# An attention stage whose order is set by tables of positions, with two stretches of value products and no mask products

## The chip, the cores and the metric

The kernel runs on one core of one Trainium2 chip. The metric is the device time of one execution in microseconds, as the median over the runs shown. A profiled execution of the same kernel gives the trace from which all rows below come.

## The reference, cut to what matters

One block of a transformer for 2048 positions of width 512 is computed, with modulation of its norms and gates by a condition vector:

```
h = layernorm(x) * (1 + ca) + sa
q, k, v = split(h @ wqkv)                 # 32 heads of 16
s = q @ k.T * 16**-0.5
s = where(0 <= i - j < 256, s, -1e9)      # i query, j key
x = x + ga * (softmax(s) @ v) @ wo
h = layernorm(x) * (1 + cb) + sb
x = x + gb * (silu(h @ w1) * (h @ w3)) @ w2
```

Each query sees itself and the 255 positions before it. With blocks of 128 positions, a query block meets three key blocks: its own (where later keys are masked), the one before it (whole), and the one before that (where only the part inside the window counts).

## The kernel before, in words

The work has three parts: a start (first norm, projections of the values, modulation), the attention, and the feed-forward part. The attention is done in 32 units. A unit `u = 4 g + b` stands for a group `g` of four heads and a block `b` of 512 positions. Each unit has three pieces, which are done for different units at the same time:

- `unit_a` projects queries and keys for unit `u`: twelve products `pj` (high and low parts of the numbers are multiplied apart, for precision), three copies out of PSUM by ScalarE (`out`), two subtractions by GpSimd (`mix`, L430), and six DMAs (`rows`) that put the parts into `ring`, the tile from which all scores are taken.
- `unit_b` finds the row maxima: sixteen products (L466, bank `mx`), each followed on VectorE by an add of a mask and a maximum in one instruction (`top`, L473), then `parts`, a `turn` on TensorE (L488), a copy (`cut`) and two DMAs that put the maxima into `ring` as further rows. The score products of `unit_c` so subtract the maximum by themselves.
- `unit_c` takes scores again with keys on the partitions: sixteen products (L717, bank `st`), for four key blocks `j`, two pairs `a` of heads and two heads `hh` in each. ScalarE exponentiates them into `pt`. Then `values_of` (L693) multiplies with the values into the bank `po`, which is copied out (L782) and stored. Since a key block serves queries of the next unit too, the products of `j` 2 and 3 have a late portion, which is done in the next unit.

There are eight PSUM banks: three `st`, three `mx`, one `pj`, one `po`.

The mask of a pair of heads is put on in one of four ways, by a letter of `MODE` at place `2 j + a`:

- E: TensorE adds the masks, by a second product of an identity with a tile of masks (L720), 256 columns wide or 128.
- D: VectorE adds the masks to the scores in PSUM (L725).
- C: VectorE copies, by a predicate, the third block's scores over the first block's masked half (`merge`, L735), since the two triangles fit together; ScalarE exponentiates two blocks instead of three (L738); GpSimd parts the merged block into two with two selects (`part`, L745).
- P: ScalarE copies the masked blocks to SBUF (`side`, L752), GpSimd masks them there (L762), ScalarE exponentiates them.

C becomes D where a key block meets fewer than three query blocks, which is so for `j` 2 and 3 at `b = 3`. The last three units take `MODL` instead of `MODE`.

The order of all steps of the attention is written by hand: every step is given a position in units of an eighth of a unit, `at(t, fn)`, and the list is sorted by position. So the positions do not set times, only the order in which each engine is given its instructions. A unit has eight positions, unit `u` of `unit_c` starts at `8 u`, `unit_a` of `u` at `8 (u - 3) + X["oa"]`, and `unit_b` at `8 (u - 2) + X["ob"]`. Beside the units run jobs (`jobs`: scaled or summed weights, a load, an operation on GpSimd, a store).

From position `TS` = 229.9 on, steps of the attention stand as fixed steps in a planner (`Sched`), which puts the work of the feed-forward part around them and behind them, by estimated durations and the keys that the constants `K` give. The planner sees the fixed steps with the durations of `KINDS`.

Of the kernel before, what the change touches and what calls it, by code (L numbers as in the profile page):

```python
# [28 lines left out]
X = dict(hh=0.184, ra=0.382, ev=(0.407, 0.03, 0.229), mix=(0.805, 0.86), row=(0.832, 0.887, 2.192), tl=0.402, mr=(0.161, 0.359, 1.088), c=(0.363, 1.109, 2.176, 0.003, 0.321, 1.738), pv=4.377, o=(0.115, 0.58), oa=-0.975, ob=1.274)  # L29
MODE = 'CECPCECP'  # L30
# [216 lines left out]
KINDS = dict(scores=("PE", 0.2), top=("DVE", 0.5), parts=("DVE", 0.4), turn=("PE", 0.11), cut=("ACT", 0.16),  # L247
# [3 lines left out]
JOB = (-1.5, 2.2, 7.9)  # L251
# [6 lines left out]
K = dict(be=(('DVE', 'POOL'), ('DVE', 'POOL'), ('DVE', 'POOL'), ('DVE', 'POOL'), ('DVE', 'POOL'),  # L258
         ('POOL', 'POOL'), ('DVE', 'POOL')), hr=9.016, de=18.699, wo=0.403, x1=3.432, xb=-3.473,
         xl=0.573, os=0.346, ol=(-6.127, -2.69, 14.829, 4.08), pl=(10.986, -0.476, -6.236,  # L260
         31.344), pe=(5.042, -12.993, 12.016, 237.531), o=(3.133, 8.773, 14.919, 2.52), n=(1, 1,
         1, 1), w0=0.71, l2=1.803, f=4.032, fl=41.71, by=((('POOL', 'POOL'), ('DVE', 'DVE'),
         ('DVE', 'POOL'), ('POOL', 'DVE')), (('POOL', 'DVE'), ('POOL', 'POOL'), ('DVE', 'POOL'),
         ('DVE', 'POOL')), (('DVE', 'DVE'), ('POOL', 'DVE'), ('POOL', 'DVE'), ('DVE', 'POOL')),
         (('POOL', 'POOL'), ('DVE', 'DVE'), ('POOL', 'POOL'), ('DVE', 'POOL'))), w=-0.242,
         dn=0.504, ds=0.172, l3=-112.914)
@with_exitstack
def block_kernel(ctx: ExitStack, tc: tile.TileContext, x, wqk, wv, wo, w13, w2, c, wmod, out):
# [183 lines left out]

    def unit_b(u, t0, at):
# [49 lines left out]
        t1 = t0 + 8 + X["tl"]
        at(t1, parts, "parts")
        at(t1 + X["mr"][0], turn, "turn")
        at(t1 + X["mr"][1], out, "cut")
        at(t1 + X["mr"][2], rows, "rows")
# [189 lines left out]
    def unit_c(u, t0, at):  # L697
# [12 lines left out]
        def scores(j, a, hh):  # L710
            kb = 4 * b + j
            nq, nm, bl = blks(j)
            if hh == 0:
# [3 lines left out]
            nc.tensor.matmul(ps[:, :nq], keys(NM, hh, a, kb, 1), queries(NM, a, kb, nq),  # L717
                             start=True, stop=not plus)
            if plus:
                nc.tensor.matmul(ps[:, bl], identr, mskr[:, :nm], start=False, stop=True)  # L720
# [740 lines left out]
    kb_ = [us(8 * (NU - NB + b) + 6 + X["pv"] + X["o"][1]) for b in range(NB)]  # L1461
# [103 lines left out]
```

## Time and profile before

| | us |
|---|---|
| median of 3 runs | 1018.6 |
| lowest, highest | 1018.1, 1021.03 |
| profiled execution | 1016.29 |
| span of the profiled execution | 1014.6 |

| engine | busy us | share of the span | instructions |
|---|---|---|---|
| TensorE (products) | 976.0 | 96% | 5432 |
| TensorE (weight loads) | 721.6 | 71% | 5432 |
| VectorE | 697.9 | 69% | 1878 |
| ScalarE | 562.3 | 55% | 1252 |
| GpSimd | 594.8 | 59% | 736 |

The mean granted clock of TensorE was 0.993. The attention lasts from about 100 to 520 us of the span; the last copy of a unit out of PSUM starts at 519.6 us. In rows of the profile PE is TensorE, PEld its weight loads, DVE VectorE, ACT ScalarE, POOL GpSimd, SP the queue that issues DMAs. A row of the timeline gives start, duration, engine, line, operation, output and inputs with their shapes, and a count; the duration of a product goes to its modelled end, so that products overlap in the rows and the distance between starts is what one takes of TensorE.

### The profile page before, as it was taken

The page shows a single profiled execution, that of the slowest core. Times are in us where ns is not written, and L with a number is a line of the kernel's source. Part 1 is how long each engine was busy: PE and PEld are TensorE (multiplying, and loading weights), DVE is VectorE, ACT ScalarE, POOL GpSimd, SP SyncE. Part 2 cuts the span into 40 slices and gives each one's busy share as a digit, 9 for nine tenths or more (in the row PEclk, how much of TensorE's full clock was granted, in tenths as well). Part 3 has the DMA queues.
Part 4 walks back from the last instruction along what each step waited for, and adds up shares of the span by engine and source line. Part 5 has one row for each costly group of instructions (what it writes and reads, how often), then busy time and mean ns, then how long its engine had stood idle before and what let it go on. Part 6 is the DMA issues. An engine that isn't in the chain of part 4 may idle for free.

```text
span 1014.6 us, 17251 instructions
## 1 busy us (share of the span) xinstructions
PE 976.0 (96%) x5432; PEld 721.6 (71%) x5432; DVE 697.9 (69%) x1878; ACT 562.3 (55%) x1252; POOL 594.8 (59%) x736
## 2 busy tenths in 40 slices
PE   5999999999999999999888899999999999999998
PEld 2578666666666666666456688878888788888886
DVE  7775777777878787878546875566577755665555
ACT  3433777777776777776557766344345444333330
POOL 7341766666665757564548677787786754433420
PEclk9999999999999999999999999999999999999999
DMA  8521353434353434335466066665556343222102
GB/s 296 161 84 43 100 173 125 143 124 144 124 173 123 143 125 148 120 134 173 161 204 221 23 239 195 219 223 193 170 162 194 130 129 93 67 84 66 49 22 83
DMA packets 79983, 141.65 MB, mean 140 GB/s; under 512 B 9234, under 2 KB 22034, under 8 KB 79764
## 3 DMA queue, kind: packets, MB, share of 16 engines
q1 hardware_dynamic: 79172, 139.50, 42.2%
q10 hardware_dynamic: 720, 1.05, 0.3%
q8 instruction: 43, 0.70, 0.3%
q14 instruction: 48, 0.39, 0.1%
HBM read 85.72 MB, written 34.61 MB: 119 GB/s over the span
## 4 chain that ended last, share of the span: by engine, by line
PE 82%; DVE 7%; ACT 4%; DMA 4%; issue 1%; POOL 1%; SPq 0%; POOLq 0%; ACTq 0%; DVEq 0%
PE st L1341 11%; PE mx L1341 11%; PE pj L412 9%; PE mx L466 9%; PE po L693 8%; PE st L717 8%; PE mx L1434 6%; PE st L1434 6%; PE st L631 4%; PE pj L1434 3%; PE pj L1341 3%; PE st L720 1%; PE mx L1079 1%; DMA o_dr<-os 1%; DVE hT L329 1%
## 5 line engine op out<-in xcount | busy, mean ns | idle before, releaser
L473 DVE CUSTOM_DVE_ANT_0 junk<-mx,mskq 128x384 bf16<-128x384 f32 (+2 forms) x512 | 267.5, 528 | 54.2 <-PE mx L466 50.4
L466 PE MATMUL mx<-ring 96*128 96x384 f32 (+2 forms) x512 | 172.9, 351 | 3.9 <-DVE mt L473 2.0
L717 PE MATMUL st<-ring 100*128 100x384 f32 (+2 forms) x512 | 157.1, 343 | 5.7 <-DMA ring<-mT 3.4
L412 PE MATMUL pj<-hT,wq 128*128 128x512 f32 x384 | 153.8, 416 | 1.5 <-DVE hT L329 1.2
L745 POOL TENSOR_SCALAR_AFFINE_SELECT pt<-pt 128x256 f32<-128x256 f32 x224 | 91.4, 413 | 94.5 <-ACT pt L738 86.8
L466 PEld LDWEIGHTS mx<-ring 96*128 96x128 f32 x512 | 94.7, 190 | 61.9 <-DVE mt L473 41.3
L934 POOL TENSOR_TENSOR w<-w,w 128x512 fp32r<-128x512 f32 (+2 forms) x56 | 98.0, 1758 | 56.5 <-ACT w L933 54.2
L738 ACT ACTIVATE pt<-st 128x256 f32<-128x256 f32 x224 | 85.4, 395 | 54.6 <-DVE st L735 53.2
L717 PEld LDWEIGHTS st<-ring 100*128 100x128 f32 x512 | 96.8, 191 | 19.4 <-ACT pt L738 6.6
L693 PE MATMUL po<-pt,vS 128*17 128x384 f32 (+2 forms) x1408 | 108.5, 393 | 0.0
L430 POOL TENSOR_TENSOR qk<-qkr,qk 128x512 fp32r<-128x512 f32 x64 | 82.3, 1286 | 42.6 <-ACT qkr L418 39.4
L729 ACT ACTIVATE pt<-st 128x384 f32<-128x384 f32 (+2 forms) x172 | 77.3, 457 | 37.8 <-PE st L720 32.9
L735 DVE COPY_PREDICATED st<-later,st 128x128 f32<-128x128 uint8 x224 | 65.2, 293 | 46.6 <-PE st L717 46.3
L412 PEld LDWEIGHTS pj<-hT,wq 128*128 128x128 f32 x384 | 72.2, 190 | 26.2 <-issue 17.8
L1372 DVE TENSOR_TENSOR t<-mx,t 128x512 f32<-128x512 f32 x51 | 35.1, 689 | 54.4 <-PE mx L1341 44.5
L1384 POOL TENSOR_TENSOR t<-t,t 128x512 f32<-128x512 f32 x28 | 36.2, 1293 | 58.6 <-DVE t L1372 56.1
L1412 ACT ACTIVATE wq<-g 128x512 fp32r<-128x512 f32 x28 | 17.7, 634 | 92.6 <-DVE g L1368 63.6
L1341 PE MATMUL st<-b,w 128*128 128x512 f32 x264 | 65.9, 392 | 0.6 <-DVE b L1238 0.6
L1372 DVE TENSOR_TENSOR t<-st,t 128x512 f32<-128x512 f32 x50 | 34.3, 688 | 45.8 <-PE st L1341 38.8
L1341 PE MATMUL mx<-b,w 128*128 128x512 f32 x258 | 63.7, 391 | 1.7 <-ACT t L1375 0.9
L1341 PEld LDWEIGHTS mx<-b,w 128*128 128x128 f32 x258 | 48.4, 188 | 12.8 <-ACT t L1375 1.3
L1341 PEld LDWEIGHTS st<-b,w 128*128 128x128 f32 x264 | 49.2, 188 | 11.5 <-DVE b L1238 1.1
(274 smaller groups left out, 2102.4 us busy)
## 6 DMA issues: line engine op xcount, KB each, us to landing
ring<-qk SPq DMA_DIRECT2D x192, 128.0 KB
o_dr<-os SPq DMA_DIRECT2D x32, 256.0 KB
w<-wsum SPq DMA_DIRECT2D x14, 512.0 KB
w<-w2g SPq DMA_DIRECT2D x14, 512.0 KB
jb<-in_w SPq DMA_DIRECT2D x24, 256.0 KB
wraw<-in_w SPq DMA_DIRECT2D x7, 768.0 KB
w<-wraw SPq DMA_DIRECT2D x14, 384.0 KB
vS<-in_wmod SPq DMA_DIRECT2D x20, 256.0 KB
```

Source lines behind the costliest of these rows:

```text
L412: nc.tensor.matmul(v["ps"], WQ[g][w][:, n // 3], hTp(i, n // 3, b * BT, BT), start=(n == 0), stop=(n == 3 * KC - 1))
L430: nc.gpsimd.tensor_tensor(out=v[n], in0=v["raw"], in1=v[1].bitcast(F32), op=ALU.subtract)
L466: nc.tensor.matmul(v[i][:, :n], queries(NS, a, gq, 1), keys(NS, hh, a, k0, gq + 1 - k0), start=True, stop=True)
L473: nc.vector.tensor_tensor_reduce(out=junk[:, :n], in0=v[i][:, :n], in1=mskq[:, 3 * P - n:], scale=1.0, scalar=-3e38, op0=ALU.add, op1=ALU. ...
L693: nc.tensor.matmul(po[32 * i:32 * i + DH + 1, qb * P:(qb + nq) * P], vS[:, kb, 4 * g + i], pts[i // 2][:, i % 2, c0:c0 + nq], start=first, ...
L717: nc.tensor.matmul(ps[:, :nq], keys(NM, hh, a, kb, 1), queries(NM, a, kb, nq), start=True, stop=not plus)
L729: nc.scalar.activation(held[u, j, a][:, hh, :nq], v[j, a, hh][:, :nq], AF.Exp, scale=SCALE)
L738: nc.scalar.activation(held[u, j, a][:, hh, :2], v[j, a, hh][:, :2], AF.Exp, scale=SCALE)
L745: nc.gpsimd.affine_select(out=pt[:, :, 2 * m], in_=pt[:, :, 0], **w)
L934: sch.op(eng, lambda: on_eng(eng).tensor_tensor(out=lo(), in0=src(), in1=hi().bitcast(F32), op=ALU.subtract), 0.06 + 0.0024 * n if eng == ...
L1341: nc.tensor.matmul(ps(bk), WT[s, n][w][:, col], BB[t, k][r], start=start and c == 0, stop=stop and c == 5, skip_group_check=True)
L1434: nc.tensor.matmul(ps(bk), tiles[hk + (h,)][:, i * P:(i + 1) * P], w2_of(last, y, f), start=(m == 0), stop=(m == 5))
```

## The change

All steps of the three pieces are placed by tables with one position for each step, in place of steps at even distances. `X` holds the tables of the attention's main part, `Y` those of the steps that are done in the start; `Y` repeats the old positions. `MODE` changes in two places: pair `j0 a1` goes from E to D, pair `j2 a1` from E to C. `MODL` stays, so the last three units keep their products L720. The products with the values of a unit stand in two groups: the late ones of the unit before together with `j` 0, and `j` 1, 2 and 3. Since the two heads of a pair can come in either order now, the tiles are taken by whichever comes first. The planner knows more of the steps (`KINDS`), waits with the tiles `qkr` and `qk` until the last rows are sent, and has new constants `K`.

```diff
-X = dict(hh=0.184, ra=0.382, ev=(0.407, 0.03, 0.229), mix=(0.805, 0.86), row=(0.832, 0.887, 2.192), tl=0.402, mr=(0.161, 0.359, 1.088), c=(0.363, 1.109, 2.176, 0.003, 0.321, 1.738), pv=4.377, o=(0.115, 0.58), oa=-0.975, ob=1.274)
-MODE = 'CECPCECP'
+X = dict(oa=-1.228, ob=1.317, wqk=(-2.382, 3.131, 4.551), pj=(-1.966, -1.918, -1.881, -0.877, -0.359, -0.355,
+         -0.265, 0.076, 1.497, 3.335, 3.917, 4.363), ev=(4.727, 5.775, 5.259), mix=(5.588, 6.021),
+         row=(8.681, 8.806, 9.018), mx=(0.546, 0.669, 1.455, 2.0, 2.064, 2.307, 2.929, 2.957, 3.255, 4.081,
+         4.688, 5.039, 6.139, 6.215, 6.787, 7.106), tl=(0.31, 0.576, 0.39, 0.716, 0.354, 0.742, 0.497, 1.151,
+         0.762, 0.785, 0.491, 0.953, 0.338, 1.726, 1.317, 1.105), mr=(8.575, 8.773, 9.063, 9.269), st=(1.873,
+         1.594, -2.503, 2.891, 0.05, 3.409, 2.644, 3.504, 4.618, 4.477, 4.419, 5.916, 5.311, 7.665, 6.691,
+         6.671), c=(0.385, 0.805, 2.402, 0.573, 0.759, 1.126), pv=(4.115, 8.948, 9.091, 9.582, 3.792, 4.101),
+         o=(9.93, 10.63), job=(-0.855, 2.493, 10.058))
+Y = dict(wqk=(0, 4, 5), pj=(0.0, 0.382, 0.764,
...
+MODE = 'CDCPCCCP'
-JOB = (-1.5, 2.2, 7.9)
-K = dict(be=(('DVE', 'POOL'), ('DVE', 'POOL'), ('DVE', 'POOL'), ('DVE', 'POOL'), ('DVE', 'POOL'),
...
+K = dict(be=(('POOL', 'DVE'), ('POOL', 'DVE'), ('DVE', 'POOL'), ('POOL', 'DVE'), ('POOL', 'DVE'),
...
-            at(t0 + n * X["ra"], lambda n=n: product(n))
+            at(t0 + y["pj"][n], lambda n=n: product(n), "product")
...
-            at(t0 + i * 0.5, lambda i=i: scores(i), "scores")
-            at(t0 + i * 0.5 + X["tl"], lambda i=i: top(i), "top")
+            at(t0 + y["mx"][i], lambda i=i: scores(i), "scores")
+            at(t0 + y["mx"][i] + y["tl"][i], lambda i=i: top(i), "top")
...
-            if hh == 0:
+            if (u, j, a) not in held:
                 held[u, j, a] = a2.tile([P, 2, 3, P], F32, name="pt", bufs=PTB)
...
-                    t = t0 + 2 * j + a + hh * X["hh"]
+                    t = t0 + X["st"][4 * j + 2 * a + hh]
...
-            at(t0 + 2 * j + X["pv"], lambda j=j: values_of(j, u), "values")
+            at(t0 + X["pv"][j], lambda j=j: values_of(j, u), "values")
         if b:
             for j in (2, 3):
-                at(t0 + X["pv"] - 1 + (j - 2) * 0.1, lambda j=j: values_of(j, u - 1), "values")
+                at(t0 + X["pv"][2 + j], lambda j=j: values_of(j, u - 1), "values")
...
+    at_ = us(8 * (NU - 4) + X["oa"] + X["row"][2]) + 3.0
+    for name in ("qkr", "qk0", "qk1", "qk2"):
+        sch.op("NIL", lambda: None, 0.0, 0.0, [], [name]).est = at_
```

More of the change, by code (lines that the diff above doesn't have):

```diff
@@ L245 @@
 TW = (231.0, 241.0, 0.8, 0.65)
-KINDS = dict(scores=("PE", 0.2), top=("DVE", 0.5), parts=("DVE", 0.4), turn=("PE", 0.11), cut=("ACT", 0.16),
+KINDS = dict(product=("PE", 0.235), mix=("POOL", 1.25), qk_rows=("SP", 1.2), out=("ACT", 0.5), job=("POOL", 2.0),
+             job_dma=("SP", 0.5), scores=("PE", 0.2), top=("DVE", 0.5), parts=("DVE", 0.4), turn=("PE", 0.11), cut=("ACT", 0.16),
              rows=("SP", 1.34), mask=("DVE", 0.33), probs=("ACT", 0.38), merge=("DVE", 0.2),
@@ L257 @@
       (("POOL", "DVE"),) * 3 + (("DVE", "DVE"),), (("POOL", "POOL"),) * 4)
-K = dict(be=(('DVE', 'POOL'), ('DVE', 'POOL'), ('DVE', 'POOL'), ('DVE', 'POOL'), ('DVE', 'POOL'),
[L259 to L266, printed above, removed]
+K = dict(be=(('POOL', 'DVE'), ('POOL', 'DVE'), ('DVE', 'POOL'), ('POOL', 'DVE'), ('POOL', 'DVE'),
+         ('POOL', 'DVE'), ('DVE', 'POOL')), hr=-0.216, de=75.767, wo=-0.032, x1=10.733,
+         xb=-11.824, xl=0.189, os=0.005, ol=(-14.872, -0.507, -6.667, 1.814), pl=(7.052, 14.678,
+         1.224, 80.012), pe=(5.061, -12.505, 27.129, 606.619), o=(10.498, 14.875, 45.043, 1.235),
+         n=(1, 1, 2, 3), w0=22.706, l2=0.337, f=29.486, fl=113.129, by=((('POOL', 'POOL'), ('DVE',
+         'POOL'), ('DVE', 'POOL'), ('DVE', 'POOL')), (('DVE', 'DVE'), ('DVE', 'POOL'), ('DVE',
+         'DVE'), ('DVE', 'POOL')), (('DVE', 'POOL'), ('DVE', 'DVE'), ('DVE', 'POOL'), ('DVE',
+         'DVE')), (('POOL', 'POOL'), ('DVE', 'DVE'), ('DVE', 'POOL'), ('POOL', 'POOL'))), w=0.573,
+         dn=0.22, ds=0.338, l3=0.286)
 @with_exitstack
@@ L441, in unit_a, with unit_b @@
             for n in range(3):
-                at(t0 + (0, 4, 5)[n], lambda n=n: load_wqk(g + 1, n))
+                at(t0 + y["wqk"][n], lambda n=n: load_wqk(g + 1, n))
         for n in range(3 * KC):
-            at(t0 + n * X["ra"], lambda n=n: product(n))
-        t1 = t0 + 3 * KC * X["ra"]
+            at(t0 + y["pj"][n], lambda n=n: product(n), "product")
         for n in range(3):
-            at(t1 + X["ev"][n], lambda n=n: out(n), "out")
-        at(t1 + X["mix"][0], lambda: mix(1))
-        at(t1 + X["mix"][1], lambda: mix(2))
+            at(t0 + y["ev"][n], lambda n=n: out(n), "out")
+        at(t0 + y["mix"][0], lambda: mix(1), "mix")
+        at(t0 + y["mix"][1], lambda: mix(2), "mix")
         for r in range(3):
-            at(t1 + X["row"][r], lambda r=r: rows(r))
-    def unit_b(u, t0, at):
+            at(t0 + y["row"][r], lambda r=r: rows(r), "qk_rows")
+    def unit_b(u, t0, at, y=X):
         g, b = divmod(u, NB)
@@ L500, in unit_b @@
         for i in range(16):
-            at(t0 + i * 0.5, lambda i=i: scores(i), "scores")
-            at(t0 + i * 0.5 + X["tl"], lambda i=i: top(i), "top")
[L503 to L507, printed above, removed]
+            at(t0 + y["mx"][i], lambda i=i: scores(i), "scores")
+            at(t0 + y["mx"][i] + y["tl"][i], lambda i=i: top(i), "top")
+        at(t0 + y["mr"][0], parts, "parts")
+        at(t0 + y["mr"][1], turn, "turn")
+        at(t0 + y["mr"][2], out, "cut")
+        at(t0 + y["mr"][3], rows, "rows")
     pre = ExitStack()
@@ L749, in side @@
             ps = v[j, a, hh]
-            if hh == 0:
+            if (j, a, "m") not in v:
                 v[j, a, "m"] = a2.tile([P, 2, 2, P], F32, name="sm", bufs=1)
@@ L887, in block_kernel @@
             for n, fn in enumerate(jobs[u]):
-                at(8 * u + JOB[n], fn)
+                at(8 * u + X["job"][n], fn, ("job_dma", "job", "job_dma")[n])
         if u in (2, 14):
@@ L1460, in block_kernel @@
     add_(0.0, lambda: load_wo(K["wo"]), "wo")
-    kb_ = [us(8 * (NU - NB + b) + 6 + X["pv"] + X["o"][1]) for b in range(NB)]
+    kb_ = [us(8 * (NU - NB + b) + X["o"][1]) for b in range(NB)]
     te, tf, fl = end, end + K["f"], K["fl"]
```

20 lines of the change are left out of this document (12 added, 8 removed).

## The prediction

> **What bounds the kernel now.** I read the page first: its busy time by engine and its chain of work that ended last.
>
> ```profile
> span 1014.6 us, 17251 instructions
> ...
> PE 976.0 (96%) x5432; PEld 721.6 (71%) x5432; DVE 697.9 (69%) x1878; ACT 562.3 (55%) x1252; POOL 594.8 (59%) x736
> ...
> PE 82%; DVE 7%; ACT 4%; DMA 4%; issue 1%; POOL 1%; SPq 0%; POOLq 0%; ACTq 0%; DVEq 0%
> ```
>
> TensorE works in 96% of the span and holds 82% of the chain. That could be an average over unlike stages, so the next view is the busy time by stretches: 16 whole units of attention, the passage to the feed-forward part, and the feed-forward part.
>
> ```profile
> core 0: us, PE busy (x) PEld busy (x) DVE busy (x) ACT busy (x) POOL busy (x), PEclk, DMA share, GB/s
> 207.71:415.63 207.92, 206.17 (x1489) 140.46 (x1490) 161.92 (x674) 154.80 (x429) 136.79 (x240) 1.00 0.42 138
> 480.00:580.00 100.00, 84.74 (x465) 57.36 (x464) 63.08 (x134) 63.74 (x131) 60.22 (x54) 0.95 0.47 159
> 580.00:1014.00 434.00, 430.10 (x1872) 348.04 (x1870) 267.64 (x356) 180.34 (x284) 244.55 (x190) 1.00 0.42 135
> ```
>
> In the 16 units (first row) TensorE is idle for 207.92 - 206.17 = 1.75 us, VectorE for 46.0, ScalarE for 53.1, GpSimd for 71.1. The passage (second row) has 15.3 us of idle TensorE, and the last 434 us only 3.9. The copy of a finished unit out of PSUM comes once per unit, so its first and last start give the period:
>
> ```profile
> L782 ACT ACTIVATE os<-po x17: 597/597/600, 207.7 to 415.6; 128x512 f32<-128x512 f32 x17
> ```
>
> 16 periods in 207.9 us are 12.99 us each. A busy TensorE is not proof of a TensorE at its rate, so I looked at its timeline, at the distance from one start to the next.
>
> ```profile
> 308.75 0.34 PE L717 MATMUL st<-ring 100*128 100x384 f32 x1
> 308.93 0.28 PE L720 MATMUL st<-mskr,identr 128*128 128x256 f32 x1
> 309.05 0.34 PE L717 MATMUL st<-ring 100*128 100x384 f32 x1
> 309.23 0.28 PE L720 MATMUL st<-mskr,identr 128*128 128x256 f32 x1
> 309.35 0.34 PE L466 MATMUL mx<-ring 96*128 96x384 f32 x1
> 309.52 0.63 PE L412 MATMUL pj<-hT,wq 128*128 128x512 f32 x2
> ...
> 310.87 0.33 PE L466 MATMUL mx<-ring 96*128 96x384 f32 x1
> 311.14 0.41 PE L693 MATMUL po<-pt,vS 128*17 128x128 f32 x8
> 311.48 0.50 PE L412 MATMUL pj<-hT,wq 128*128 128x512 f32 x1
> 311.82 0.34 PE L466 MATMUL mx<-ring 96*128 96x384 f32 x1
> 312.00 0.39 PE L412 MATMUL pj<-hT,wq 128*128 128x512 f32 x1
> 312.23 0.52 PE L717 MATMUL st<-ring 100*128 100x384 f32 x2
> ```
>
> Distances between starts: scores 384 wide 0.18 (308.75 to 308.93), a mask product 256 wide 0.12 (308.93 to 309.05), the maxima's scores 384 wide 0.18 (311.82 to 312.00), a projection 512 wide 0.23 (312.00 to 312.23). TensorE goes from one product to the next at a pace set by their widths. The exception is a stretch of products with the values (L693, 128*17): before it the distance is 0.27 instead of 0.18 (310.87 to 311.14), and after it the next product but one starts 0.34 after the next one, although a projection takes 0.23 elsewhere (311.48 to 311.82). So this stage is set by the sum of TensorE's starts, with a loss at each entry to and exit from the values.
>
> **The change, part by part.** All terms are per unit, then times the units.
>
> *Mask products (L720) go in the first 29 units.* The second products of the pairs marked E were:
>
> ```profile
> L720 PE MATMUL st<-mskr,identr x64: 223/282/286, 211.1 to 413.2; 128*128 128x256 f32 x56, 128*128 128x128 f32 x8
> ```
>
> 64 of them in 16 units, 56 of 256 columns (0.12 each, above) and 8 of 128 (half): 7.2 us, 0.45 us per unit. They lie on the path, since nothing else fills TensorE. The last three units keep them.
>
> *Two stretches of values in place of five.* Before, units had the positions 3.377 and 3.477 (the late products of the previous unit, adjacent), 4.377, 6.377, 8.377, 10.377, with other products between: five stretches, four where b is 0, so 76 in 16 units. After, late j2, late j3 and j0 stand at 3.792, 4.101, 4.115, and j1, j2, j3 at 8.948, 9.091, 9.582. I sorted the new tables: no TensorE step falls inside either group (mx5 at 3.624 and mx6 at 4.246; mx15 at 8.423 and st at 9.594). So 32 stretches in 16 units, 44 fewer. The number of products stays (704 in the 16 units):
>
> ```profile
> L693 PE MATMUL po<-pt,vS x704: 272/379/499, 209.9 to 415.3; 128*17 128x384 f32 x64, 128*17 128x256 f32 x56, 128*17 128x128 f32 x56
> ```
>
> One stretch costs 0.27 - 0.18 = 0.09 at entry and 0.34 - 0.23 = 0.11 one product after exit. The exit itself is 0.34 (311.14 to 311.48) for 8 products one block wide. I take 0.10 of it for the exit, because the entry and the product after cost the same; bounds 0 and 0.2. That is 0.30 per stretch (0.2 to 0.4), times 44: 13.2 us, 0.83 us per unit (0.55 to 1.1). The waits view shows the entry alone, summed over most stretches, where the weight load waits on TensorE itself:
>
> ```profile
> PEld mx L466 <- DVE mt L473: 19.7, 35, 0.6
> ...
> PEld po L693 <- issue: 16.1, 65, 0.3
> ```
>
> The Trainium skill, TensorEngine Tiling (Array Packing), Key Properties, says that a change of tiling mode drains TensorE; a matmul of 17 columns placed by quarters against one of 128 is such a change. The trace agrees as far as it shows a loss of about 0.1 us on either side. By that rule alone, read as only one drain on entry and one on exit, the saving would be 44 x 0.2 = 8.8 us in place of 13.2, an estimate.
>
> *VectorE gets work.* Per unit two masks 128x256 (pair j0a1) and, where b is not 3, two more merges; where b is 3 two adds of 128x128. What such instructions take, start to start:
>
> ```profile
> 304.92 0.30 DVE L725 TENSOR_TENSOR st<-st,mskr 128x128 f32<-128x128 f32 x1
> 305.12 0.55 DVE L473 CUSTOM_DVE_ANT_0 junk<-mx,mskq 128x384 bf16<-128x384 f32 x1
> ...
> 305.59 0.55 DVE L473 CUSTOM_DVE_ANT_0 junk<-mx,mskq 128x384 bf16<-128x384 f32 x1
> ...
> 307.63 0.29 DVE L735 COPY_PREDICATED st<-later,st 128x128 f32<-128x128 uint8 x1
> 307.83 0.55 DVE L473 CUSTOM_DVE_ANT_0 junk<-mx,mskq 128x384 bf16<-128x384 f32 x1
> ```
> ```profile
> L735 DVE COPY_PREDICATED st<-later,st 128x128 f32<-128x128 uint8 x113 | 33.1, 293 | 16.5 <-PE st L717 16.4
> ```
>
> A 128-wide add costs 0.20 (304.92 to 305.12), a merge 0.20, and a row maximum 384 wide 0.47. The 256-wide add is not in the trace: it lies between 0.20 and 0.47, and I take 0.33, its place by width. So 2 x 0.33 + 2 x 0.20 = 1.06 us per unit, and VectorE's busy time goes from 161.92/16 = 10.12 to 11.18 us. That is under 12.99 and beside TensorE; at a period of 12.0 the cover is 0.8 us per unit, and no more. I cost it at nothing directly and put its risk into the waits below. The units with b = 1 and 2 have all of it; those with b = 0 have narrower maxima.
>
> *ScalarE and GpSimd.* ScalarE's exponentials of pair j2a1 shrink from 384 to 256 wide, and GpSimd gets two selects for it:
>
> ```profile
> L738 ACT ACTIVATE pt<-st 128x256 f32<-128x256 f32 x112 | 42.9, 396 | 25.0 <-DVE st L735 24.3
> L729 ACT ACTIVATE pt<-st 128x384 f32<-128x384 f32 x56 | 28.0, 499 | 16.2 <-PE st L720 16.1
> ```
> ```profile
> L745 POOL TENSOR_SCALAR_AFFINE_SELECT pt<-pt 128x256 f32<-128x256 f32 x112 | 45.1, 408 | 40.6 <-ACT pt L738 36.8
> ```
>
> ScalarE: -2 x 0.1 us. GpSimd: +0.82 us in 12 of 16 units, from 136.79/16 = 8.55 to 9.2 us. Neither fills a unit of 12 us.
>
> The Trainium skill, SBUF — State Buffer, Who interferes with whom, speaks against adding to both at once: GpSimd and VectorE share a port pair, and the loser blocks for a whole instruction, unless VectorE's instruction has at most one SBUF input. Masks and merges here have one operand in PSUM, and the selects ran beside a VectorE busy for 78% without a spread:
>
> ```profile
> L762 POOL TENSOR_SCALAR_AFFINE_SELECT sm<-sm x109: 405/408/415, 106.5 to 475.5; 128x256 f32<-128x256 f32 x109
> ```
>
> 405 to 415 ns over 109 selects: no blocking is seen. Were each new select blocked for one row maximum, GpSimd would get 0.94 us more per unit, 10.1, still under 12.
>
> *Order, and the waits that it may make.* Two chains got shorter cover. (1) Score j3a0h1 at 7.665 must be merged, exponentiated and parted before the values of j3 at 9.582; before, j3a0 stood at 6.18 and its values at 10.377. TensorE's work in between is st, st, mx14, pj8, mx15 (0.18 x 4 + 0.23), entry 0.09 and the values of j1 and j2, three and two blocks at 0.24 each: 2.2 us. The chain is 0.34 (product) + 0.29 (merge) + 0.40 + 2 x 0.41 = 1.85 us, plus up to 0.47 behind a row maximum and 0.5 behind another exponential: between 0.35 early and 0.6 late. I take 0.2 late. What waits then is the whole of TensorE. (2) The rows of the next unit: the second mix ends, two row DMAs are issued, and they must land before mx0. Before:
>
> ```profile
> 302.50 2.64 POOL L430 TENSOR_TENSOR qk<-qkr,qk 128x512 fp32r<-128x512 f32 x2 [0.97 <-ACT qkr L418]
> ```
> ```profile
> 301.38 4.97 SPq L435 DMA_DIRECT2D ring<-qk  x6
> ```
>
> The mixes ended at 305.14, and mx0 started at 309.35 (above), 4.2 us later. After, mix and mx0 stand 5.07 positions apart instead of 4.80, which at 1.50 us instead of 1.62 us per position is 7.6 for 7.8, and a part (0.82) comes between the two mixes: 3.2 us are left. Two issues of at most 0.83 leave 1.5 for landing. No such wait stands among the 16 units now, so a landing takes less than 4.2 - 1.7 = 2.5: a stall of 0 to 1.0 us. On SP the load of the next job now stands ahead of these rows; its buffer was stored five positions earlier, so it should not hold the queue. I take 0.1 for all this, nearest to the row without a wait. Tiles of probabilities live up to 8.9 positions instead of 7.4, and with nine buffers the ninth next use still comes after the release. The maxima's banks, released by VectorE (35 waits, 19.7 us of weight loads in the view above, mostly under running products), I leave as they are.
>
> *Start, end and feed-forward.* The start uses Y, which repeats the old positions: nothing. The planner's constants K are all new; products stay the same. In the passage these waits are on the path:
>
> ```profile
> 474.14 4.25 DMA ring<-qk
> ```
> ```profile
> 478.61 0.58 PE L466 MATMUL mx<-ring 96*128 96x384 f32 x2 [1.51 <-DMA ring<-qk]
> ...
> 499.86 0.58 PE L717 MATMUL st<-ring 100*128 100x384 f32 x2 [3.39 <-DMA ring<-mT]
> ```
>
> At most the 15.3 us of idle could go; a loss I bound by one more of each wait, 1.5 + 3.4 = 5 us. I take zero.
>
> **Sum.** Gain per unit 0.45 + 0.83 - 0.20 - 0.10 = 0.98, a period of 12.0 us. 28 periods of units with the new modes give 27.4; the first unit and the last three, which are held by DMAs as the rows above show, I count with 2.5 together. 30 us less than the profiled execution's 1016.3 (span 1014.6) is 986.3. The median of the runs is 1018.6, 2.3 above: 988.
>
> **The rivals.**
> - *TensorE bound, and the waits do not grow* (1.28 per unit, perhaps 0.2 of old waits gone too): 36 to 44 us less, 975 to 983. For it: every hand-off of banks that I walked through came before its use. Against: chain (1).
> - *VectorE starves in the stretches.* For 1.5 us TensorE gives it nothing; three banks of maxima hold 1.4 us of work. If 0.4 to 0.7 us are lost per unit, the gain is 8 to 18 us: 1000 to 1010.
> - *Slower: VectorE bounds the stage.* Its idle time per unit is now 46.0/16 = 2.88 us. If the in-order queue keeps that idle time, the period is 11.18 + 2.88 = 14.06, 1.07 longer, 30 us in 28 units: 1048. It decides as soon as the idle time stays above 12.99 - 11.18 = 1.81 us. The forecast needs it to fall to 0.8. For it: VectorE waits on TensorE's scores now, in small pieces. Against: it waits because TensorE is late, and TensorE gets faster. The Trainium skill, Perfetto Trace Analysis, Identifying the Most-Contended Engine, judges TensorE by weight-load time rather than busy time; that is 140.46 of 207.92, 68%, under VectorE's 78%, so by that page VectorE is the engine to relieve and this change loads it. The distances between starts speak against that reading here.
> - *The new passage takes back or doubles the gain*: within the range unless above 10 us.
>
> **How the numbers follow.** Forecast 0.50 (980 to 995), no growth of waits 0.17, starved VectorE 0.17, slower (VectorE or late rows) 0.10, a passage that eats the gain 0.06, of which half ends within 0.3% (3 us, about what a measurement of this kernel can tell from no change). Faster 0.85, same 0.04, slower 0.11. The range 972 to 1008 leaves out the slower case, the passage case and a tail of the starved one, and a little below.
>
> **What would show it.** Period of the copies out of PSUM 11.8 to 12.2 us; mask products 140 down to 24 (three units of eight); about 0.09 to 0.1 us lost at each of two stretches; VectorE busy above 90% of a unit. Wrong if weight loads of the values wait on GpSimd's parts (chain 1), if mx0 waits on the rows' DMA (chain 2), if TensorE's idle time per unit rises over 0.5 us on VectorE's maxima, or if the stretch from 480 to 580 is much longer than 100 us.

## The result, and the profile after

The changed kernel takes 992.73 us (median of 4 runs, 991.36 to 997.54) against 1018.35 us of the kernel before: a ratio of 0.9754, 95% interval 0.9715 to 0.9793. It is 25.6 us faster; 30 were forecast. The profiled execution took 992.91 us.

From the page of the changed kernel, the span, the busy times and the chain that ended last by engine:

```profile
span 991.2 us, 17139 instructions
...
PE 945.8 (95%) x5316; PEld 719.7 (73%) x5316; DVE 719.6 (73%) x1998; ACT 552.8 (56%) x1252; POOL 604.6 (61%) x776
...
PE 74%; DMA 8%; DVE 7%; POOL 4%; ACT 3%; issue 2%; SPq 1%; POOLq 0%; DVEq 0%; ACTq 0%
```

TensorE's share of the chain fell from 82% to 74%; DMA's rose from 4% to 8%. Next the busy time by stretches, with the columns of the prediction's view: 16 units (from the 3rd to the 19th copy out of PSUM), the last four units, and the rest.

```profile
core 0: us, PE busy (x) PEld busy (x) DVE busy (x) ACT busy (x) POOL busy (x), PEclk, DMA share, GB/s
137.96:328.49 190.53, 187.82 (x1425) 136.77 (x1425) 172.25 (x736) 151.57 (x428) 144.73 (x266) 1.00 0.45 149
436.80:497.15 60.35, 47.27 (x319) 30.70 (x320) 34.57 (x118) 33.20 (x89) 29.66 (x46) 0.89 0.49 152
497.15:991.20 494.05, 480.95 (x2086) 386.19 (x2085) 311.62 (x427) 217.70 (x356) 279.10 (x211) 1.00 0.41 138
```

The 16 units take 190.5 us, 11.91 us each instead of 12.99: 1.09 us less per unit. VectorE is busy for 172.25 us in them, 90%, and idle for 1.14 us per unit instead of 2.88. (Its busy time is 10.77 us per unit, not the 11.18 of the prediction. Where rows overlap, busy time counts the time once. The durations of the rows add up to 14.05 us per unit here and to 14.25 in e1, below, which has the same work and the 11.18; so more of them overlap here.) The same last two stretches of the kernel before:

```profile
467.18:519.64 52.46, 45.45 (x316) 26.80 (x317) 31.46 (x104) 32.80 (x85) 29.71 (x43) 0.93 0.55 176
519.64:1014.60 494.96, 480.27 (x2083) 385.35 (x2082) 309.78 (x427) 220.84 (x356) 282.28 (x214) 1.00 0.42 138
```

From the copy of unit 27 to that of the last unit the kernel before took 52.46 us and the changed kernel 60.35, 7.9 us more; the rest takes 0.9 us less. So the account is: 3.4 us gained up to the first copy (117.3 to 113.9), 27.0 from there to unit 27, minus 7.9, plus 0.9: 23.4 us, the difference of the two spans.

The steps that the prediction named can be seen one by one. The mask products that are left, by their line in the changed kernel:

```profile
L731 PE MATMUL st<-mskr,identr x24: 224/283/418, 443.3 to 493.1; 128*128 128x256 f32 x20, 128*128 128x128 f32 x4
```

24 instead of 140. One of the two stretches of values on TensorE's timeline:

```profile
211.91 0.33 PE L478 MATMUL mx<-ring 96*128 96x384 f32 x1
212.17 1.49 PE L704 MATMUL po<-pt,vS 128*17 128x128 f32 x24
```

All 24 products of three key blocks stand in one row, with an entry of 0.26 (211.91 to 212.17). And the add of 256 columns, which the trace before did not have, with the row maximum behind it on VectorE:

```profile
211.48 0.43 DVE L736 TENSOR_TENSOR st<-st,mskr 128x256 f32<-128x256 f32 x1
211.82 0.55 DVE L485 CUSTOM_DVE_ANT_0 junk<-mx,mskq 128x384 bf16<-128x384 f32 x1
```

0.34 from start to start (0.33 was taken). From the waits of the 16 units (who waited for whom, total, times, longest):

```profile
DVE junk L485 <- PE mx L478: 12.6, 27, 1.1
...
PEld po L704 <- POOL pt L756: 7.0, 18, 0.7
...
POOL sm L773 <- DMA ring<-qk: 2.6, 2, 1.3
```

VectorE waits less for TensorE than before (12.6 us in 190.5 against 23.4 in 207.9), and the values wait a little for GpSimd's parts, 18 times. In the last row the profile puts two waits of GpSimd down to the rows' DMA. TensorE's own wait for these rows, chain (2) of the prediction, does not show in the 16 units. It shows in others: 0.38 us at 114.55, 0.61 at 329.41 and 1.81 at 378.45, in a unit of 13.65 us.

What went against the change is in SP's queue at the passage, and on TensorE behind it:

```profile
441.89 0.44 SPq L1020 DMA_DIRECT2D wo<-wog  x1
442.37 1.69 SPq L1042 DMA_DIRECT2D wqr<-o_dr  x2
444.16 7.94 SPq L448 DMA_DIRECT2D ring<-qk  x6
```
```profile
454.21 0.66 PE L478 MATMUL mx<-ring 96*128 96x384 f32 x1 [5.25 <-DMA ring<-qk]
...
477.95 0.66 PE L728 MATMUL st<-ring 100*128 100x384 f32 x1 [4.56 <-DMA ring<-mT]
```

The load of the output projection's weights, 1 MB, and two loads of stored outputs were issued ahead of the last unit's six row DMAs. These took 7.94 us to issue, and TensorE waited 5.25 us for them (1.51 before), then 4.56 us for the next maxima (3.39 before). One wait of the queue itself is 3.2 of the 7.94 us:

```profile
SPq L448 <- DMA wo<-wog: 3.2, 1, 3.2
```

The sixth row DMA was issued when the load of the weights had landed. In the trace the DMAs of this queue take eight semaphores (the counters that tell of a landing) in turn, and the sixth row DMA is the eighth behind the load, so it takes the load's. In the kernel before the load stood ahead of the last rows too, but directly, so that none of them took its semaphore:

```profile
468.97 0.44 SPq L1010 DMA_DIRECT2D wo<-wog  x1
469.75 4.97 SPq L435 DMA_DIRECT2D ring<-qk  x6
```

There they took 4.97 us, as in most units of that kernel. The two named waits grew by 4.9 us together; from unit 28's copy to the last TensorE is idle for 7.0 us more than before (12.1 against 5.1) and busy for 2.7 us more, at a mean granted clock of 0.86 against 0.92.

### The profile page after: what moved, and what is told of

It is laid out like the page before. It is cut to its first block, busy times and chain, and to the rows that moved or that the text cites. A ratio compares the mean times of both kernels' runs of the same rounds, so it can differ in the third digit from the quotient of the medians.

```text
span 991.2 us, 17139 instructions
## 1 busy us (share of the span) xinstructions
PE 945.8 (95%) x5316; PEld 719.7 (73%) x5316; DVE 719.6 (73%) x1998; ACT 552.8 (56%) x1252; POOL 604.6 (61%) x776
## 3 DMA queue, kind: packets, MB, share of 16 engines
q10 hardware_dynamic: 720, 1.05, 0.3%
## 4 chain that ended last, share of the span: by engine, by line
PE 74%; DMA 8%; DVE 7%; POOL 4%; ACT 3%; issue 2%; SPq 1%; POOLq 0%; DVEq 0%; ACTq 0%
PE mx L1351 12%; PE st L1351 11%; PE mx L478 7%; PE pj L425 7%; PE st L728 7%; PE st L1444 6%; PE mx L1444 6%; PE po L704 6%; PE st L642 4%; PE pj L1351 3%; PE pj L1444 2%; DMA o_dr<-os 2%; POOL pt L756 2%; POOL qk L443 1%; DMA ring<-qk 1%
## 5 line engine op out<-in xcount | busy, mean ns | idle before, releaser
L485 DVE CUSTOM_DVE_ANT_0 junk<-mx,mskq 128x384 bf16<-128x384 f32 (+2 forms) x512 | 256.6, 527 | 38.4 <-PE mx L478 36.9
L478 PE MATMUL mx<-ring 96*128 96x384 f32 (+2 forms) x512 | 155.8, 342 | 11.8 <-DMA ring<-qk 8.0
L756 POOL TENSOR_SCALAR_AFFINE_SELECT pt<-pt 128x256 f32<-128x256 f32 x268 | 109.4, 411 | 72.5 <-ACT pt L749 61.9
L425 PE MATMUL pj<-hT,wq 128*128 128x512 f32 x384 | 136.7, 406 | 0.6 <-DVE hT L342 0.6
L749 ACT ACTIVATE pt<-st 128x256 f32<-128x256 f32 x268 | 96.1, 386 | 38.8 <-DVE st L746 30.8
L704 PE MATMUL po<-pt,vS 128*17 128x384 f32 (+2 forms) x1408 | 95.9, 389 | 1.2 <-POOL pt L756 0.8
L443 POOL TENSOR_TENSOR qk<-qkr,qk 128x512 fp32r<-128x512 f32 x64 | 82.8, 1293 | 17.6 <-ACT qkr L431 17.3
L704 PEld LDWEIGHTS po<-pt,vS 128*17 128x17 f32 x1408 | 33.1, 97 | 46.6 <-issue 21.1
L740 ACT ACTIVATE pt<-st 128x384 f32<-128x384 f32 (+2 forms) x128 | 53.2, 434 | 23.2 <-DVE st L736 13.3
L1378 DVE TENSOR_TENSOR g<-t,g 128x512 f32<-128x512 f32 x42 | 56.6, 1353 | 5.8 <-POOL t L1394 4.5
L773 POOL TENSOR_SCALAR_AFFINE_SELECT sm<-sm 128x256 f32<-128x256 f32 x109 | 41.9, 407 | 28.2 <-ACT sm L763 24.3
```

Of the source, the lines that this page charges most:

```text
L425: nc.tensor.matmul(v["ps"], WQ[g][w][:, n // 3], hTp(i, n // 3, b * BT, BT), start=(n == 0), stop=(n == 3 * KC - 1))
L443: nc.gpsimd.tensor_tensor(out=v[n], in0=v["raw"], in1=v[1].bitcast(F32), op=ALU.subtract)
L478: nc.tensor.matmul(v[i][:, :n], queries(NS, a, gq, 1), keys(NS, hh, a, k0, gq + 1 - k0), start=True, stop=True)
L485: nc.vector.tensor_tensor_reduce(out=junk[:, :n], in0=v[i][:, :n], in1=mskq[:, 3 * P - n:], scale=1.0, scalar=-3e38, op0=ALU.add, op1=ALU. ...
L704: nc.tensor.matmul(po[32 * i:32 * i + DH + 1, qb * P:(qb + nq) * P], vS[:, kb, 4 * g + i], pts[i // 2][:, i % 2, c0:c0 + nq], start=first, ...
L749: nc.scalar.activation(held[u, j, a][:, hh, :2], v[j, a, hh][:, :2], AF.Exp, scale=SCALE)
```

## The experiments

| kernel | median us | ratio to before, 95% interval | us per unit (16 units) |
|---|---|---|---|
| before | 1018.35 | 1 | 12.99 |
| changed | 992.73 | 0.9754, 0.9715 to 0.9793 | 11.91 |
| e1 modes alone | 1042.18 | 1.0251, 1.0209 to 1.0292 | 14.09 |
| e2 stretches alone | 1032.73 | 1.0159, 1.0122 to 1.0197 | 13.25 |
| e3 masks back | 997.93 | 0.9826, 0.9777 to 0.9875 | 12.19 |
| e4 last rows early | 1003.88 | 0.9862, 0.9814 to 0.9910 | 11.88 |
| e5 values spread | 1038.28 | 1.0190, 1.0175 to 1.0206 | 13.24 |
| e6 old constants | 997.44 | 0.9810, 0.9783 to 0.9837 | 11.90 |
| e7 add undone | 994.41 | 0.9766, 0.9730 to 0.9801 | 12.12 |
| e8 fewer products | 988.27 | 0.9698, 0.9679 to 0.9717 | 11.88 (8 units), 12.14 (16) |
| e9 load behind rows | 987.25 | 0.9690, 0.9674 to 0.9706 | 11.87 |
| e10 narrow maxima | 989.84 | 0.9726, 0.9709 to 0.9744 | 11.88 |
| e11 both relieved | 983.00 | 0.9658, 0.9625 to 0.9691 | 11.79 |
| e12 loads behind rows | 989.25 | 0.9727, 0.9705 to 0.9749 | 11.90 |

Each was run beside the kernel before, whose medians in the four groups lay between 1016.8 and 1019.2. The last column is of one profiled execution: before, e1 and e2 from the 8th to the 24th copy, the others from the 3rd to the 19th, where before has 12.98, e1 13.97 and e2 13.32. The changed kernel, e4, e6, e9 and e12 are alike in these units; their periods, 11.87 to 11.91, show how far executions differ.

### The parts alone, in the old order

```diff
-MODE = 'CECPCECP'
+MODE = 'CDCPCCCP'
```

> The kernel before, with the letters of MODE alone changed: pair j0 a1 masked by VectorE, pair j2 a1 merged and parted, order and five stretches as before. Theory A (the sum of TensorE's starts sets the stage): the mask products of 29 units go, 29 x 0.45 = 13 us less, about 1005 us. Theory B (hand-offs over VectorE and GpSimd set it, and the new order alone brings the gain): VectorE's 1.06 us more per unit eats the saving, 1015 us or more.

25 us slower, as theory B has it. The windows row of 16 units of e1, in the columns of the table above, and the wait that became the largest on TensorE:

```profile
213.79:439.30 225.51, 206.68 (x1425) 134.24 (x1426) 178.94 (x738) 154.61 (x429) 145.20 (x263) 0.98 0.39 127
```
```profile
PE mx L488 <- DVE mr L482: 16.4, 16, 1.7
```

VectorE is busy for 178.94/16 = 11.18 us per unit, to the digit what the prediction gave, and idle for 2.91 us, as before (2.88). The period is their sum, 14.09. The maxima of a unit come late, and their turn on TensorE waits about 1 us in each of the 16 units. In the old order the 1.06 us given to VectorE made the unit 1.10 us longer.

```diff
-            at(t0 + 2 * j + X["pv"], lambda j=j: values_of(j, u), "values")
+            at(t0 + (3.48, 10.3, 10.35, 10.377)[j], lambda j=j: values_of(j, u), "values")
```

> The kernel before, with the positions of the value products alone changed: late j2, late j3 and j0 together at 3.377 to 3.48, j1, j2 and j3 together at 10.3 to 10.377; mask products stay. Theory A: 44 stretches fewer in 16 units at 0.30 each, 0.83 us per unit, 26 us in 32 units, about 992 us. With the loss read as one drain at entry and one at exit, 0.2 each, 18 us, about 1000 us. Theory B: a stretch of 1.5 us starves VectorE, and its waits take back half or more: 1005 us or more.

16 us slower, theory B again. Windows of 16 units and VectorE's wait:

```profile
211.72:423.70 211.98, 206.81 (x1489) 145.41 (x1490) 158.71 (x672) 154.48 (x428) 136.53 (x239) 1.00 0.41 135
```
```profile
DVE junk L473 <- PE mx L466: 28.0, 32, 1.5
```

VectorE waits for scores 32 times, twice per unit, 28.0 us in all, 0.9 us for each stretch (before, 65 shorter waits, 23.4 us). Its idle time rises from 2.88 to 3.33 us per unit. If the stretches that went saved the 0.83 us of the prediction, the two long ones cost 1.08; TensorE's busy time (206.81 us, 206.17 before) shows no saving.

So neither part is worth anything in the old order; each makes the kernel slower.

### The parts taken out of the new order

```diff
-MODE = 'CDCPCCCP'
+MODE = 'CECPCECP'
```

> The changed kernel, with the letters of MODE put back: tables and two stretches stay, the mask products return to TensorE, VectorE and GpSimd lose the added work. Theory A: 13 us more, about 1006 us. Theory B (VectorE or GpSimd bound the changed kernel): no more than 3 us more, 993 to 996 us.

5.2 us slower than the changed kernel by the medians (the intervals of the two ratios overlap), between the two theories, and 12.19 us per unit:

```profile
138.03:333.04 195.01, 193.84 (x1489) 144.80 (x1490) 162.67 (x673) 153.39 (x428) 136.42 (x243) 1.00 0.45 147
```

The mask products are worth 0.28 us per unit in the new order, not 0.45. VectorE is idle for 2.0 us per unit here and TensorE for 0.07, so TensorE seems to set the unit, and without the products VectorE to take part. Most of the gain, 0.80 of 1.09 us per unit, is there with the masks on TensorE.

```diff
-MODE = 'CDCPCCCP'
+MODE = 'CECPCCCP'
```

> The changed kernel, with pair j0 a1 masked by TensorE again; pair j2 a1 stays merged. TensorE gets 0.24 us more per unit, VectorE 0.66 us less. If TensorE's starts set the stage now: 29 x 0.24 = 7 us more, about 1000 us. If VectorE limits the changed kernel: up to 19 us less, 975 to 988 us. If both are near the limit: no change, 990 to 995 us.

994.41 us: no difference that the runs can tell from the changed kernel, which was expected for the case that both engines are near the limit. The period is 12.12, 0.21 longer, for 0.24 us more on TensorE, although VectorE is relieved by 0.4 us:

```profile
137.98:331.94 193.96, 191.42 (x1457) 140.81 (x1457) 165.69 (x705) 149.49 (x428) 145.10 (x267) 1.00 0.45 148
```

```diff
-pv=(4.115, 8.948, 9.091, 9.582, 3.792, 4.101)
+pv=(4.45, 7.2, 8.948, 9.7, 3.5, 3.6)
```

> The changed kernel, with the value products spread again: late j2 and j3 at 3.5 and 3.6, j0 at 4.45, j1 at 7.2, j2 at 8.948, j3 at 9.7, five stretches, all else of the new order kept. If each stretch costs TensorE 0.30 us and TensorE's starts set the stage: 0.83 us per unit more, 26 us, about 1019 us; with 0.2 per stretch 1011 us. If hand-offs set the stage and long stretches starve VectorE, spreading costs little: 1001 us or less.

46 us slower than the changed kernel, past both theories, and 1.33 us more per unit. The edit makes more stretches than was meant: a score product stands at 3.504, between the late j2 at 3.5 and the late j3 at 3.6, so the trace has 88 stretches in the 16 units, not 76. That is 56 more than in the changed kernel, 3.5 per unit, 1.05 us at 0.30 each.

```profile
141.21:353.09 211.88, 205.19 (x1425) 131.79 (x1426) 176.37 (x737) 153.86 (x428) 145.15 (x267) 1.00 0.41 135
```

TensorE's busy time rises by 17.4 us, 0.31 for each of the 56 stretches, near the 0.30 of the prediction, though busy time can hold waits too. VectorE is idle for 35.5/16 = 2.22 us per unit, against 1.14. The new tables were made for two stretches; with five or six, the entries and exits come back and VectorE waits more as well. This edit moves j1 and j3 against their data too, so the causes are not told apart by size.

### What bounds the changed kernel

```diff
-        for n in range(3 * KC):
+        for n in (range(3 * KC) if y is Y else [n for n in range(3 * KC) if n % 3 != 1]):
```

> The changed kernel, with four of the twelve projections of queries and keys left out in 29 units (one of the three products of high and low parts). TensorE gets 0.93 us less per unit, no other engine changes. If TensorE's starts set the stage: 27 us less, about 966 us. If VectorE (11.2 us busy in a unit of 11.9) or the hand-offs set it: 10 us less or fewer, 983 us or more.

4.5 us less than the changed kernel, of the 27 if TensorE's starts set the stage. Eight units of e8, and the same eight of the changed kernel:

```profile
136.96:232.00 95.04, 92.22 (x681) 61.02 (x681) 85.93 (x369) 74.78 (x215) 72.30 (x136) 1.00 0.45 146
```
```profile
137.96:232.67 94.71, 93.80 (x713) 68.54 (x713) 85.79 (x368) 75.78 (x215) 73.07 (x137) 1.00 0.44 147
```

95.04 against 94.71 us: with 0.93 us less of work on TensorE the unit is as long as before. (Over 16 units e8 has one unit of 16.45 us, which the eight leave out. In it TensorE waits 1.84 us for the rows, among whose DMAs a job's load, `wqr`, had been issued: chain (2) of the prediction.) The 4.5 us lie in the last four units, 55.8 us instead of 60.35, where the last rows were not held (below). The busy time of TensorE fell by 1.6 us, though 8 x 0.93 = 7.4 us of products went. A product 384 wide is a row of 0.34 us, and the next can start 0.18 us behind it; so a pause of up to 0.16 us behind it counts as busy.

```diff
-SCALE = DH ** -0.5
+SCALE = DH ** -0.5 / 4
...
+            lo = 64 if n == 3 * P and y is X else 0
-                out=junk[:, :n], in0=v[i][:, :n], in1=mskq[:, 3 * P - n:], scale=1.0, scalar=-3e38,
+                out=junk[:, lo:n], in0=v[i][:, lo:n], in1=mskq[:, 3 * P - n + lo:], scale=1.0, scalar=-3e38,
```

> The changed kernel, with VectorE relieved: the row maxima in the main part read 320 of their 384 columns (the first 64 are left out, and the exponents are scaled down to a quarter, which keeps them finite). VectorE gets about 0.9 us less per unit, 64 columns at the slope of 0.47 us for 384 in 14 of 16 maxima. If VectorE alone limits the changed kernel: 25 us less, about 968 us. If TensorE and VectorE are both full, as e8 with TensorE relieved suggests (4.5 us less): 5 us less or fewer, 987 us or more.

2.9 us less, of the 25 if VectorE alone sets the unit:

```profile
137.57:327.68 190.11, 186.48 (x1425) 137.39 (x1425) 161.21 (x736) 151.72 (x429) 144.68 (x267) 1.00 0.46 151
```

VectorE's busy time fell by 11 us in 16 units, and the period by 0.03 us. So VectorE alone does not set it either.

The edits of e8 and e10 together:

> The changed kernel, with both reliefs: the narrower maxima with scaled exponents, and four of twelve projections left out in 29 units. If TensorE and VectorE are both full in the changed kernel: 0.9 us less per unit, 20 to 26 us less, 967 to 973 us. If GpSimd or the chains of single tiles set the unit: 10 us less or fewer, 983 us or more.

9.7 us less, where two full engines alone would give 20 to 26: the second theory, by which GpSimd or the chains of single tiles set the unit. From the first copy to unit 27's e11 takes 7.5 us less than the changed kernel, while e8 takes 0.5 more and e10 1.0 less; so the two reliefs work together. The windows of 16 units, and the chain by line in them:

```profile
135.95:324.51 188.56, 181.70 (x1361) 123.60 (x1362) 161.44 (x736) 150.03 (x428) 144.53 (x267) 0.99 0.47 152
```
```profile
by line: POOL pt L757 15.4%; PE mx L478 14.3%; PE st L729 13.5%; PE po L705 12.2%; POOL qk L443 11.4%; issue 7.7%; PE pj L425 7.1%; POOL sm L774 5.5%; DMA ring<-qk 3.2%; ACT pt L750 2.0%; DMA wqr<-g_dr 2.0%; DVE st L747 1.5%; POOL wq L413 1
```

By line GpSimd's parts (L757) now lead with 15.4%, and the mixes (L443) have 11.4%; TensorE's four lines together still have more, 47.1%. Four units of the changed kernel one by one show where GpSimd is full:

```profile
149.85:161.38 11.53, 11.53 (x78) 8.46 (x79) 11.07 (x47) 9.57 (x28) 8.49 (x17) 1.00 0.43 141
161.38:173.65 12.27, 12.10 (x94) 8.73 (x95) 11.60 (x48) 10.05 (x29) 9.17 (x19) 1.00 0.44 151
173.65:185.22 11.57, 11.57 (x94) 8.58 (x94) 9.72 (x47) 9.48 (x27) 10.47 (x20) 1.00 0.46 150
185.22:197.64 12.42, 11.84 (x94) 8.42 (x95) 10.88 (x46) 8.72 (x26) 8.37 (x14) 1.00 0.42 142
```

The third has TensorE busy throughout, VectorE for 84% and GpSimd for 10.47 of 11.57 us. (It is not one of the longer ones; the first is as short with 8.49 us of GpSimd.) Its GpSimd timeline goes from one instruction to the next:

```profile
175.26 0.88 POOL L756 TENSOR_SCALAR_AFFINE_SELECT pt<-pt 128x256 f32<-128x256 f32 x2
176.11 1.28 POOL L413 TENSOR_TENSOR wq<-wqr,wq 128x512 fp32r<-128x512 f32 x1
177.34 0.77 POOL L773 TENSOR_SCALAR_AFFINE_SELECT sm<-sm 128x256 f32<-128x256 f32 x2
178.07 1.30 POOL L443 TENSOR_TENSOR qk<-qkr,qk 128x512 fp32r<-128x512 f32 x1
```

175.26, 176.11, 177.34, 178.07: each starts as the one before it ends. This is the unit in which GpSimd also subtracts the weights of the next group (L413) and sums a job (L854). It comes once in four units, and it is 11.57 us long in e11 too. So neither TensorE nor VectorE sets the unit alone. Over the 27 periods from the first copy to unit 27's the changed kernel and those like it there take 11.88 to 12.00 us per unit; e8 with 11.98 and e10 with 11.92 cannot be told from them, and e11 takes 11.68. In the 16 units e11 gains 0.12 us per unit, with one unit of 14.04 us among them in which TensorE again waited for the rows. That GpSimd takes part, in every fourth unit, is read from its timeline and not shown by a run: a kernel that relieves GpSimd was not run, and the chains of single tiles are a rival that stays open.

### The passage

```diff
-            at(t0 + y["row"][r], lambda r=r: rows(r), "qk_rows")
+            at(t0 + ((6.9, 6.95, 7.05)[r] if u == NU - 1 else y["row"][r]), lambda r=r: rows(r), "qk_rows")
```

> The changed kernel, with the row DMAs of the last unit alone put ahead of position 229.9, so that they stand in SP's queue ahead of the planner's first loads. If those loads made TensorE wait 5.25 us for the rows of the last unit, the wait falls to 1 us or less and the time by 4 to 6 us, about 988 us. If the passage is set by the chain from the stored outputs to the feed-forward part, the wait goes and comes back later: 991 to 994 us.

11 us slower than the changed kernel, outside both ranges, and the wait stays at 5.3 us. The planner set its loads ahead of the rows again:

```profile
442.43 0.43 SPq L1020 DMA_DIRECT2D wo<-wog  x1
442.96 5.94 SPq L448 DMA_DIRECT2D ring<-qk  x6
```

The chain has the weights' load from 442.43 on for 10.08 us. The edit also made the planner deal all later work anew; in the stretch from the last copy to 560 us TensorE is idle for 15.3 us instead of 8.5, with a granted clock of 0.78 instead of 0.97. So this run tells little of the rows, and much of how a plan reacts to a small edit. The next kernel kept the plan and moved one DMA in the finished order:

```diff
+    behind = max(i for i, f in enumerate(order) if f in LATE_ROWS)
+    first = order.index(WO_LOAD[0])
+    order.insert(behind, order.pop(first))
```

> The changed kernel, with one DMA issued later: the load of the output projection's weights (1 MB) stands behind the row DMAs of the last unit instead of ahead of them; the planner's order is the same otherwise. If that transfer holds the rows: TensorE's wait of 5.25 us for the last unit's rows falls to 2 us or less, and the time by 3 to 5 us, about 988.5 us. If the transfers of the passage as a whole set it, or something later does: 991 to 994 us.

987.25 us, 5.5 less than the changed kernel, and the interval of its ratio lies below that of the changed kernel. SP's queue, and TensorE's waits for DMAs in the last units:

```profile
441.77 3.88 SPq L448 DMA_DIRECT2D ring<-qk  x6
445.70 0.59 SPq L1021 DMA_DIRECT2D wo<-wog  x1
```
```profile
PE st L728 <- DMA ring<-mT: 6.5, 1, 6.5
PE mx L478 <- DMA ring<-qk: 1.3, 1, 1.3
```

The six row DMAs are issued in 3.88 us instead of 7.94, none of them behind the load's semaphore, and the wait falls from 5.25 to 1.3 us. The wait for the next maxima rises from 4.56 to 6.5. From the copy of unit 27 to the end, e9 takes 551.5 us against 554.4:

```profile
434.56:986.10 551.54, 526.31 (x2404) 415.50 (x2404) 346.67 (x545) 251.51 (x444) 308.16 (x257) 0.99 0.43 141
```

So 2.9 us of the 5.5 lie where the edit is; the other part of the profiled difference lies ahead of it, where the kernels are alike. e9 is the fastest of the versions that leave nothing out.

A load ahead of the rows does not hold them always. e8 has the queue of the changed kernel, load first, and issues the rows in 3.88 us:

```profile
442.29 0.43 SPq L1020 DMA_DIRECT2D wo<-wog  x1
444.55 3.88 SPq L448 DMA_DIRECT2D ring<-qk  x6
```

There the load had landed 5.49 us after its issue, just as the sixth row DMA came to its turn; in the changed kernel it took 9.65. Why the load takes longer in one kernel than in the other is not shown.

```diff
-    first = order.index(WO_LOAD[0])
-    order.insert(behind, order.pop(first))
+    early = [f for f in order[:behind] if f in WO_LOAD]
+    order[:behind + 1] = [f for f in order[:behind + 1] if f not in early] + early
```

> As e9, with the loads of x that stood ahead of the last unit's rows issued behind them too. If what is left of the wait for the rows (1.3 us) comes from those loads: 1 us less than e9, about 986 us. If they only move the contention to the next rows, those of the maxima (6.5 us of wait in e9): 987 to 992 us.

989.25 us: not better than e9. Its span is 986.3 us against 986.1. TensorE's wait for the rows is gone, and the wait for the next maxima is 6.2 us: the second theory. The interval of e12, which holds e9's edit too, overlaps that of the changed kernel.

```diff
-K = dict(be=(('POOL', 'DVE'), ('POOL', 'DVE'), ('DVE', 'POOL'), ('POOL', 'DVE'), ('POOL', 'DVE'),
...
+K = dict(be=(('DVE', 'POOL'), ('DVE', 'POOL'), ('DVE', 'POOL'), ('DVE', 'POOL'), ('DVE', 'POOL'),
...
```

> The changed kernel, with the planner's constants K of the kernel before. If the new constants are worth something with the new tables: 5 us more or worse, 998 us or more. If the tail's loss of 9.7 us against the kernel before comes from the new constants: 5 to 10 us less, 983 to 988 us. Neither: 990 to 995 us.

4.7 us slower than the changed kernel by the medians, just short of the first theory's 998, with intervals that overlap. The last units and the rest:

```profile
434.67:487.33 52.66, 44.54 (x306) 27.47 (x307) 32.87 (x114) 33.03 (x89) 29.23 (x46) 0.90 0.52 169
487.33:996.10 508.77, 487.55 (x2099) 392.65 (x2097) 302.92 (x427) 221.77 (x357) 284.91 (x215) 0.97 0.41 135
```

With the old constants the attention ends 10 us earlier (52.66 us for the last four units, as before the change), and the rest takes 14.7 us longer. The load stands ahead of the last rows here too, but lands before the rows need its semaphore, and they take 3.87 us to issue. So the 7.9 us that the tail lost come with the new plan, nearly all of them, and the new plan pays them back behind the attention.

## Why the prediction was right, and where it was not

**The sum.** Forecast 0.98 us per unit, measured 1.09; from the first copy to unit 28's, 28 periods, 28.8 us against 27.4. (30 us less than 1018.6 is 988.6; the prediction wrote 988.) The median is 4.7 us above the forecast, because of one term. In the spans the units gave 1.4 us more than forecast, the term below 8.8 us less, and the rest 0.9 more.

**The term that was mis-sized** is the passage with the last three units. The prediction took zero for the passage, bounded its loss by 5 us, and took the first unit and the last three together as a gain of 2.5. Measured: plus 3.4 in the first, minus 9.7 from unit 28's copy to the last (38.8 us before, 48.5 after). The rows' late place in the order was seen for the steady units (chain 2), and no wait of that kind rules them, though it shows in single units. But in the last unit the rows' late place meets the new plan: the weights' load stands eight DMAs ahead of the sixth row DMA, which takes the load's semaphore and stood until it had landed. With the load behind the rows (e9) they are not held, and with the old constants (e6) the tail takes 52.7 us, as before the change. The two waits that the prediction named grew by 4.9 us, within its bound of 5. The rest of the 9.7 is other idle time of TensorE and 2.7 us more of busy time, at the lower granted clock given above.

**The terms of the steady units came out near as a sum, and their reason was wrong.** "They lie on the path, since nothing else fills TensorE" was said of the mask products (0.45), and the stretches (0.83) were counted in the same way, each by itself. e1 and e2 refute it: each alone makes the kernel slower, by 1.10 and 0.26 us per unit. In the kernel before, TensorE was idle for 0.11 us per unit and VectorE for 2.88; but VectorE's idle time could not be used in the old order. The rival "VectorE bounds the stage", with a period of 14.06, came true in e1: 14.09 us over the same 16 units, and 13.97 from the 3rd to the 19th copy. What turned it into the forecast is the order: the tables alone with two stretches and the old modes (e3) bring 0.80 of the 1.09, and with the masks moved VectorE's idle time falls to 1.14. The masks bring 0.28, not 0.45. How the 0.80 divides between the two stretches and the rest of the new order, no run shows: e5 changes both. So it is in part luck that 0.45 + 0.83 - 0.30 came within 0.11 us of the measured gain. The prediction had the right test, "the forecast needs it to fall to 0.8": VectorE's idle time came to 1.14, nearer to 0.8 than to the 1.81 at which the change turns into a loss. That the new order would bring it down had only been walked through by hand.

**Waits.** The prediction let them grow by 0.30 us per unit. Against its two gains, 1.28 - 1.09 = 0.19 is missing; as the masks brought less than their term, this is not a measure of the waits. Chain (1) shows in weight loads of the values that wait for parts (18 times, 7.0 us), mostly under running products: of TensorE's own waits 0.2 us are put down to parts in the 16 units, where the prediction had 0.2 in each. Chain (2) shows in single units, 2.8 us in 28 of them, the 0.1 per unit that the prediction had.

**GpSimd** was dismissed ("neither fills a unit of 12 us"). On the mean that holds, 9.05 us per unit. In the unit with the weights' subtraction it does not: there GpSimd runs through, busy for 10.47 of 11.57 us.

**The ranking that was put aside.** The Trainium skill, Perfetto Trace Analysis, Identifying the Most-Contended Engine, judges TensorE by its weight loads (and by MFU) and not by its busy time; by the weight loads VectorE comes first here. The prediction set the distances between starts against it. These were read rightly, and yet e1 agrees with the page: 1.06 us more on VectorE cost 1.10 per unit. e8 agrees too, as TensorE's busy time hides waits there.

## What to carry to other kernels

Where two in-order engines hand banks to each other, a sum of one engine's work prices a change only together with the order that lets the other engine keep up: ask how much of the other's idle time the order can use, unit by unit. Look at the fullest unit of each engine and not only the mean. And where a written order meets a planner's, look at what stands ahead of the last critical DMA in the queue, and at the semaphore for which that DMA waits: one load of 1 MB moved behind it brought about 3 us where it was made.

## What the runs showed of the hardware

TensorE's busy time in the profile does not fall with its work: four of twelve projections left out took 7.4 us of work from eight units and 1.6 us of busy time. And the time from a DMA's issue to its landing is not a constant of its size: the load of 1 MB took 9.65 us in the changed kernel and 5.49 in e8, from the same place in the queue.
